# Three rows of w2 loaded ahead of the first K unit, and b1 loaded in one transfer, in a one-core decode kernel

## The chip, the cores and the metric

The kernel runs on one core of a Trainium2 chip. The metric is device time in microseconds (us). The kernel before takes 134.15 us (median of 5 runs, 134.06 to 134.36). A run of this program is called slow when it is over 1.5% above the fastest run of the same kernel; verdicts use the other runs, called fast. A change of under 2% counts as "same", so everything below is about tenths of a microsecond.

## The reference

x is normalised; an attention over the last 2048 cached positions (16 K/V heads, two batch rows, one query position) and a feed-forward part with a squared ReLU both read the normalised x; their results and x are added.

```python
xn = _layernorm(x, axis=-1)
return x + _A_ref(xn, A_k_cache, A_v_cache, A_wq, A_wo) + _B_ref(xn, B_w1, B_b1, B_w2, B_b2)
# _A_ref: q = xn @ wq; softmax(q k^T / sqrt(Dh)) v; @ wo       x is [2, 1, 576], Dh = 128
# _B_ref: h = xn @ w1 + b1; out = max(h, 0)^2 @ w2 + b2        w1 [576, 4608], w2 [4608, 576]
```

All of it is one position per batch row, so 53.6 MB of caches and weights pass through the core once, with little arithmetic on each byte.

## The kernel before

K and V come in eight units of 2 MB each; all large loads are issued by SyncE (`nc.sync`), the few small ones by ScalarE. w2's 4608 rows lie in four groups of 9 rows per partition. The parts that matter:

```python
    def issue_kv(tiles, cache, u, name, parts=1):      # [128 x 8192]: 32 x 4 pieces of DRAM
        tl = kvpool.tile([P, UE], BF16, tag="kv", name=f"{name}_{u}")
        v = unit_view(cache, u)
        ...                                            # nc.sync.dma_start(out=tl[...], in_=v[...])
    def issue_w2(g, r0, r1):
        if r0 == 0:
            w2_rows[g] = kvpool.tile([P, FR * D], BF16, tag="kv", name=f"w2_{g}")
        tl = w2_rows[g][:, r0 * D:r1 * D]
        rows = B_w2[g * HW:(g + 1) * HW, :].rearrange("(p r) n -> p (r n)", r=FR)
        nc.sync.dma_start(out=tl, in_=rows[:, r0 * D:r1 * D])
        ...

    nc.scalar.dma_start(out=x_sb[0:B, :], in_=x2d)
    for g in range(2):
        nc.scalar.dma_start(out=b1_sb[2 * g:2 * g + 2, :], in_=...)      # b1, two transfers
    for i in range(2):
        nc.scalar.dma_start(out=x_sb[B:B + 1, ...], in_=...)             # b2, two transfers
    ...
    for f in issue_kv(k_tiles, A_k_cache, 0, "k"):     # the first load of SyncE: K0
        f()
    issue_w(A_wq, "wq", QL)
    ...
    load_k(1); load_v(0); issue_w(B_w1, "w1", FL); load_k(2); load_v(1); load_k(3)
    for g in range(NG):
        transposes(0, g)                               # TensorE: K0
    q_all()                                            # TensorE: q = xn @ wq; frees wq's buffer for w1
    ...                                                # units 1 to 7
    W2P = [(0, 0, 9), (1, 0, 9), (2, 0, 9), (3, 0, 7), (3, 7, 9)]        # the last loads
    for w in W2P:
        issue_w2(*w)
    ...
    mlp_tail(*W2P[NG4][1:])                            # ends 3 us after the last load has landed
```

Of the kernel before, what the change touches and what calls it, by code (L numbers as in the profile page):

```python
# [8 lines left out]
F32 = mybir.dt.float32  # L9
BF16 = mybir.dt.bfloat16  # L10
# [6 lines left out]
def kernel(  # L17
# [14 lines left out]
    nc = tc.nc  # L32
    P = 128
    B, Sq, D = A_x.shape
# [24 lines left out]
    NG4 = 4  # L59
# [4 lines left out]
    HW = F // NG4  # L64
    HB = HW // 3
    FR = HW // P
# [7 lines left out]
    const = ctx.enter_context(tc.tile_pool(name="const", bufs=1))  # L74
# [7 lines left out]
    def pe_mm(out, **kw):  # L82
        return tc.keep_in_program_order(nc.tensor.matmul(out, **kw))  # L83
# [10 lines left out]
    k_tiles, v_tiles, w_tiles, wo_tiles, w2_tiles = {}, {}, {}, {}, {}  # L94

    def unit_view(cache, u):
        tq, b = divmod(u, B)
        return cache[b, tq * TH:(tq + 1) * TH, S0:Sk, :].rearrange("h (c j) d -> c h (j d)", c=CP)

    def issue_kv(tiles, cache, u, name, parts=1):  # L100
        tl = kvpool.tile([P, UE], BF16, tag="kv", name=f"{name}_{u}")
        v = unit_view(cache, u)
        n = UE // parts
        tiles[u] = tl
        return [lambda i=i: nc.sync.dma_start(out=tl[:, i * n:(i + 1) * n], in_=v[:, :, i * n:(i + 1) * n])  # L105
                for i in range(parts)]
# [7 lines left out]
    def issue_wo(t):  # L114
        if t == 0:
            wo_tiles["all"] = wbig.tile([P, B * WR, D], BF16, tag="wbig", name="wo_sb")
        tl = wo_tiles["all"][:, t * WR:(t + 1) * WR, :]
        n = P * WR
        nc.sync.dma_start(out=tl, in_=A_wo[t * n:(t + 1) * n, :].rearrange("(p r) n -> p r n", r=WR))
        wo_tiles[t] = tl  # L120
# [3 lines left out]
# [6 lines that stand above are left out]
        w2_tiles[(g, r0)] = tl  # L130
# [1 line left out]
    x_sb = const.tile([B + 1, D], BF16, name="x_sb")  # L132
    nc.scalar.dma_start(out=x_sb[0:B, :], in_=x2d)
    b1_sb = const.tile([NG4, HW], BF16, name="b1_sb")
    for g in range(2):
        nc.scalar.dma_start(out=b1_sb[2 * g:2 * g + 2, :], in_=B_b1[2 * g * HW:2 * (g + 1) * HW].rearrange("(g n) -> g n", g=2))
    for i in range(2):
        nc.scalar.dma_start(out=x_sb[B:B + 1, i * OH:(i + 1) * OH],
                            in_=B_b2[i * OH:(i + 1) * OH].rearrange("(o n) -> o n", o=1))
    eps_t = const.tile([B, 1], F32, name="eps_t")  # L140
    nc.vector.memset(eps_t[:], 1e-5)
    warm = const.tile([B, 122], F32, name="warm")
    nc.scalar.activation(out=warm[:, 0:1], in_=eps_t[:], func=ACT.Sqrt)
    for f in issue_kv(k_tiles, A_k_cache, 0, "k"):
        f()
    issue_w(A_wq, "wq", QL)
# [37 lines left out]
    for a in range(2):  # L184
        for r in range(NR2):
# [3 lines left out]
                          in_=pro_ps[:, 0:2 * NR2, :].rearrange("p (a r) b -> p r a b", a=2))  # L189
    nc.vector.tensor_copy(out=xnT[:, 1:HP:2, :, :],  # L190
                          in_=pro_ps[:].rearrange("p (a r) b -> p r a b", a=2)[:, 0:NR2 - 1, :, :])
# [16 lines left out]
                          in_=ident[0:TH, 0:TH].unsqueeze(1).to_broadcast([TH, NT * 32 // TH, TH]))  # L208
    par = const.tile([P, 2, 2, Dh // 2], BF16, name="par")
    for e in range(2):  # L210
        nc.gpsimd.tensor_copy(out=par[:, e, :, :],
                              in_=ident[:, e:Dh:2].unsqueeze(1).to_broadcast([P, 2, Dh // 2]))
# [3 lines left out]
    for k in range(2):  # L216
        for h in range(2):
            a = (h + k) % 2 * B
# [4 lines left out]
                          in_=ident[0:NG4, 0:NG4].unsqueeze(2).to_broadcast([NG4, NG4, B]))  # L223
# [6 lines left out]
    def out_acc(lhsT, rhs_of, start=False, stop=False):  # L230
        for i in range(2):
            pe_mm(out_ps[32 * i:32 * i + B, :], lhsT=lhsT, rhs=rhs_of(i * OH, (i + 1) * OH),
                  start=start, stop=stop, skip_group_check=True)
# [132 lines left out]
    def pv_out(u):  # L366
        tq, b = divmod(u, B)
        t, half = divmod(tq, 2)
        if u % (2 * B) == 0:
            sm_tiles[t] = psum.tile([P, B, Dh + 1], F32, tag="sm", name=f"sm_{t}")  # L370
        sm = sm_tiles[t]
        pe_mm(sm[half * (P // 2):(half + 1) * (P // 2), b, :],
                         lhsT=tohead[:].rearrange("p c x -> p (c x)"), rhs=acc_tiles.pop(u)[:], start=True, stop=True,
                         skip_group_check=True, tile_position=(0, half * (P // 2)))
        if u % (2 * B) == 2 * B - 1:
            ri = work.tile([P, B], F32, tag="ri", name=f"ri_{t}")
            pin(nc.vector.reciprocal(out=ri[:], in_=sm[:, :, Dh]))
            od = work.tile([P, B, DW, WR], F32, tag="od", bufs=1, name=f"od_{t}")
            for k in range(B):
                nc.vector.scalar_tensor_tensor(out=od[:, k, :, :],  # L380
                                               in0=sm[:, k, 0:Dh].rearrange("p (x r) -> p x r", x=DW),
                                               scalar=ri[:, k:k + 1],
                                               in1=own[:].unsqueeze(2).to_broadcast([P, DW, WR]),
                                               op0=ALU.mult, op1=ALU.mult)
            ws = work.tile([P, WR, B], BF16, tag="ws", name=f"ws_{t}")
            with nc.allow_low_precision(reason="sums of one value and zeros"):
                nc.vector.tensor_reduce(out=ws[:], in_=od[:].rearrange("p b x r -> p r b x"), axis=AX.X, op=ALU.add)  # L387
            wo_state[t] = ws

    def wo_acc(tq):  # L390
        ws = wo_state.pop(tq)
        wo_sb = wo_tiles.pop(tq)
        for r in range(WR):
            out_acc(ws[:, r, :], lambda a, z: wo_sb[:, r, a:z])

    mlp = {}
# [40 lines left out]
    def mlp_o(g, r0, r1):  # L437
        w2_sb = w2_tiles.pop((g, r0))
        for r in range(r0, r1):
            o = (r - r0) * D  # L440
            out_acc(mlp["h"][:, g * FR + r, :], lambda a, z: w2_sb[:, o + a:o + z], stop=(g == NG4 - 2 and r == r1 - 1))

    part = const.tile([B, D], F32, name="part")

    def mlp_tail(r0, r1):
        w2_sb = w2_tiles.pop((NG4 - 1, r0))
        for r in range(r0, r1):
            o = (r - r0) * D
            for i in range(4):
                pe_mm(mlp["out"][32 * i:32 * i + B, :], lhsT=mlp["h"][:, (NG4 - 1) * FR + r, :],  # L450
                                 rhs=w2_sb[:, o + i * OQ:o + (i + 1) * OQ], start=False, stop=(r == FR - 1),
                                 skip_group_check=True, tile_position=(0, 32 * i))

    def load_k(u):
        for f in issue_kv(k_tiles, A_k_cache, u, "k"):
            f()

    def load_v(u):
        for f in issue_kv(v_tiles, A_v_cache, u, "v"):
            f()  # L460

    W2P = [(0, 0, 9), (1, 0, 9), (2, 0, 9), (3, 0, 7), (3, 7, 9)]

    load_k(1)
    load_v(0)
# [13 lines left out]
    def step(u, p=None, o=None):  # L479
        if p is not None:  # L480
            pv_start(p)
        transposes(u, 0)
        softmax_max(u - 1)
        transposes(u, 1)
        softmax_exp(u - 1)
        transposes(u, 2)
        if p is not None:
            pv(p, 0)
        transposes(u, 3)
        if p is not None:  # L490
            pv(p, 1)
        softmax_tr(u - 1)
        if o is not None:
            pv_out(o)
        transposes(u, 4)
        scores(u, 0)
        for g in range(GW + 1, NG):
            transposes(u, g)
        for i in range(2, NR):
            if p is not None:  # L500
                pv(p, i)
        if p is not None:
            pv_mix(p)
        scores(u, 1)
# [13 lines left out]
    for u in range(2, NU - 1):  # L518
        step(u, u - 2 if u > 2 else None, u - 3 if u > 2 else None)
        if u == 2:  # L520
            out_acc(res_b[:], lambda a, z: x_sb[:, a:z], start=True)
        if u + 1 < NU - 1:
            load_v(u + 1)
        if u == 4:
            issue_wo(0)
        if u + 3 < NU:
            load_k(u + 3)
        if u == 5:
            load_v(NU - 1)
    issue_wo(1)  # L530
    for w in W2P:
        issue_w2(*w)
# [11 lines left out]
    wo_acc(0)  # L544
    pv_out(NU - 1)
    mlp_o(*W2P[0])
    wo_acc(1)
    for w in W2P[1:NG4 - 1]:
        mlp_o(*w)
# [3 lines left out]
    for i in range(4):  # L553
        pe_mm(mlp["out"][32 * i:32 * i + B, :], lhsT=ident_f[0:B, 0:B], rhs=part[:, i * OQ:(i + 1) * OQ],
              start=True, stop=False, skip_group_check=True, tile_position=(0, 32 * i))
    mlp_tail(*W2P[NG4 - 1][1:])
    mlp_tail(*W2P[NG4][1:])

# [36 lines left out]
```

## Time and profile before

| | before |
|---|---|
| time, median of 5 | 134.15 us |
| span of the profiled run | 132.2 us |
| first packet of a large load | 2.13 us |
| marks of K0 / wq / V0, median of 16 | 7.97 / 18.89 / 28.70 us |
| marks of the last load: first, median, last | 127.22, 127.89, 129.09 us |
| from the last mark to the end of the span | 3.1 us |

A load is split over 16 DMA engines, and each sends a completion mark when its share has landed. The trace holds the time of each mark and the start, size and duration of each packet, but it does not say which engine a mark or packet belongs to. The spread of a load's 16 marks shows how far the engines are apart. The lines of the profile are in the prediction. Here is only the head, which the argument turns on, in stretches of half a microsecond; the last two columns are the DMA share and GB/s, with each packet counted where it starts:

```profile
1.60:2.10 0.50, 0.00 (x0) 0.00 (x0) 0.39 (x2) 0.00 (x0) 0.50 (x3) 1.00 0.04 5
2.10:2.60 0.50, 0.00 (x0) 0.00 (x0) 0.40 (x3) 0.03 (x1) 0.50 (x1) 1.00 1.84 492
2.60:3.10 0.50, 0.00 (x0) 0.00 (x0) 0.49 (x3) 0.50 (x1) 0.34 (x1) 1.00 0.08 33
3.10:3.60 0.50, 0.00 (x0) 0.00 (x0) 0.44 (x4) 0.50 (x1) 0.00 (x0) 1.00 1.24 524
```

Until 2.1 us only x moves (5 GB/s). Then 15 of the 16 engines start one large K packet each (492), and in the next stretch only the last of them does (33), because those first packets take about 1 us instead of 0.61.

### The profile page before, as it was taken

To read this page: it belongs to the slowest core of one execution; us is meant where nothing else is said; L and a number is where in the kernel's file an instruction comes from. 1 tells how busy PE (TensorE), PEld (TensorE's weight loads), DVE (VectorE), ACT (ScalarE), POOL (GpSimd) and SP (SyncE) were. 2 spreads that over 40 slices of the span, in tenths; PEclk is the share of its full clock that TensorE was granted. 3 is DMA by queue.
4 is the path that set the end of the run, shared out by engine and by line. 5 is a ranking of instruction groups with operands and counts; after the bars stand their busy time and mean duration, and the time that the engine had idled before them with its cause. 6 is when DMAs were issued, how large, how long until landed. Compare 5 with 4: busy or idle time off the path is not lost.

```text
span 132.2 us, 2040 instructions
## 1 busy us (share of the span) xinstructions
PE 89.0 (67%) x830; PEld 54.7 (41%) x830; DVE 59.1 (45%) x150; ACT 44.2 (33%) x64; POOL 7.7 (6%) x26
## 2 busy tenths in 40 slices
PE   0069319789862967879889389789303996399761
PEld 0059202639521354744466064466003661155540
DVE  6944400224640019246675823778800358644011
ACT  2705401015700226438457145357100751200011
POOL 7700000001000001000010000010000000000000
PEclk9999995955999599689999977999985699959999
DMA  4999989999998999999999999999999999999950
GB/s 154 389 451 479 413 382 431 431 484 477 439 404 350 436 416 441 426 446 416 431 431 426 436 421 439 426 429 431 428 441 416 446 423 422 429 420 433 419 238 1
DMA packets 3632, 53.74 MB, mean 406 GB/s; under 512 B 412, under 2 KB 420, under 8 KB 680
## 3 DMA queue, kind: packets, MB, share of 16 engines
q1 hardware_dynamic: 3604, 53.61, 95.2%
q8 instruction: 6, 0.10, 0.3%
q10 hardware_dynamic: 20, 0.01, 0.0%
q14 instruction: 2, 0.02, 0.0%
HBM read 53.62 MB, written 0.00 MB: 405 GB/s over the span
## 4 chain that ended last, share of the span: by engine, by line
DMA 72%; PE 20%; DVE 2%; ACT 2%; issue 1%; SPq 1%; DVEq 0%; ACTq 0%
DMA k<-in_A_k_cache_dram 44%; DMA w<-in_B_w_dram 14%; DMA wq_sb<-in_A_wq_dram 13%; PE kT_ps L86 10%; PE sc_ps L83 4%; PE q_ps L83 3%; PE pv_ps L83 2%; PE qs_ps L83 1%; DVE kT L286 1%; ACT kT L284 1%; ACT pr L323 1%; PE sm L83 1%; DVE qrow L250 1%; SPq L105 0%; DVE qz L266 0%
## 5 line engine op out<-in xcount | busy, mean ns | idle before, releaser
L86 PE MATMUL kT_ps<-ident_f,k 128*128 128x128 f32 x256 | 41.4, 319 | 12.6 <-DMA k<-in_A_k_cache_dram 12.1
L284 ACT COPY kT<-kT_ps 128x1024 bf16<-128x1024 bf16 x32 | 31.9, 1011 | 36.8 <-PE kT_ps L86 34.0
L86 PEld LDWEIGHTS kT_ps<-ident_f,k 128*128 128x128 f32 x256 | 34.4, 165 | 21.9 <-issue 16.6
L286 DVE COPY kT<-kT_ps 128x1024 bf16<-128x1024 bf16 x32 | 22.1, 691 | 31.9 <-PE kT_ps L86 31.8
L83 PE MATMUL sc_ps<-kT,qz 128*32 128x512 bf16 x128 | 10.7, 418 | 4.5 <-DVE kT L286 2.8
L83 PE MATMUL pv_ps<-v,pT 128*32 128x512 bf16 x128 | 11.7, 435 | 1.0 <-DVE acc L358 0.8
L312 POOL PARTITION_ALL_REDUCE gmax<-m x8 | 2.9, 365 | 103.1 <-DVE m L310 103.1
L323 ACT ACTIVATE pr<-sc_ps,nb 128x512 bf16<-128x512 f32 x8 | 5.5, 687 | 7.9 <-DVE nb L320 7.9
L83 PEld LDWEIGHTS <-xnT 128*4 128x4 bf16 x90 | 2.9, 105 | 11.6 <-issue 11.0
L308 DVE TENSOR_REDUCE mx<-sc_ps 128x1 f32<-128x512 f32 x8 | 5.5, 683 | 3.1 <-PE sc_ps L83 3.1
L83 PE MATMUL q_ps<-wq_sb,xnT 128*4 128x512 bf16 x36 | 3.7, 592 | 4.5 <-DMA wq_sb<-in_A_wq_dram 4.5
L83 PEld LDWEIGHTS <-qz 128*32 128x32 bf16 x128 | 2.3, 98 | 10.1 <-DVE kT L286 6.3
L83 PE MATMUL h_ps<-w_sb,xnT 128*4 128x384 bf16 x54 | 3.9, 420 | 3.4 <-DMA w_sb<-in_B_w_dram 3.4
L358 DVE SCALAR_TENSOR_TENSOR mix<-pv_ps,own_j,mix 128x128 f32<-128x128 f32 x16 | 5.6, 352 | 0.6
L329 DVE STREAM_TRANSPOSE pT<-pr 128x512 bf16<-128x512 bf16 x8 | 5.6, 702 | 0.2 <-ACT pr L323 0.2
L86 PE MATMUL pro_ps<-ident,xs 2*128 2x2 bf16 x10 | 0.6, 164 | 7.6 <-DVE xs L180 7.6
L83 PE MATMUL out_ps<-wo_sb,ws 128*2 128x288 bf16 x64 | 5.1, 323 | 0.3 <-DVE ws L387 0.3
L83 PEld LDWEIGHTS <-pT 128*32 128x32 bf16 x128 | 2.9, 98 | 5.9 <-issue 3.5
L551 ACT COPY part<-out_ps 2x288 f32<-2x288 f32 x1 | 0.4, 389 | 13.5 <-PE out_ps L83 13.5
L83 PE MATMUL sm<-acc,tohead 128*64 128x129 f32 x16 | 3.7, 313 | 1.8 <-DVE acc L358 1.8
L431 DVE TENSOR_TENSOR hs<-hT_ps,hodd 128x20 f32<-128x20 f32 (+1 forms) x4 | 0.5, 172 | 9.2 <-ACT hodd L428 9.2
L83 PE MATMUL out_ps<-w,hT_sb 128*2 128x288 bf16 x54 | 3.8, 286 | 1.1 <-DMA w<-in_B_w_dram 1.1
(78 smaller groups left out, 58.2 us busy)
## 6 DMA issues: line engine op xcount, KB each, us to landing
k<-in_A_k_cache_dram SPq DMA_DIRECT2D x8, 2048.0 KB, 7.7
v<-in_A_v_cache_dram SPq DMA_DIRECT2D x8, 2048.0 KB, 16.9
w_sb<-in_B_w_dram SPq DMA_DIRECT2D x1, 5184.0 KB, 19.3
wq_sb<-in_A_wq_dram SPq DMA_DIRECT2D x1, 4608.0 KB
wo_sb<-in_A_wo_dram SPq DMA_DIRECT2D x2, 2304.0 KB
w<-in_B_w_dram SPq DMA_DIRECT2D x3, 1296.0 KB, 27.2
w<-in_B_w_dram SPq DMA_DIRECT2D x1, 1008.0 KB
w<-in_B_w_dram SPq DMA_DIRECT2D x1, 288.0 KB
```

What stands on the lines that cost most here:

```text
L83: return tc.keep_in_program_order(nc.tensor.matmul(out, **kw))
L86: return tc.keep_in_program_order(nc.tensor.transpose(**kw))
L250: nc.vector.tensor_copy(out=qrow[:, 0, :], in_=q_ps[0][0:RB, :])
L284: pin(nc.scalar.copy(out=dst, in_=src))
L286: pin(nc.vector.tensor_copy(out=dst, in_=src))
L308: pin(nc.vector.tensor_reduce(out=mx[:], in_=sc_ps, axis=AX.X, op=ALU.max))
L312: nc.gpsimd.partition_all_reduce(gmax[:], m2[:], channels=P, reduce_op=ReduceOp.max)
L323: pin(nc.scalar.activation(out=pr[:], in_=sc_ps, func=ACT.Exp, bias=nb[:], scale=scale, accum_out=acc[:, Dh:Dh + 1]))
L329: pin(nc.vector.transpose(out=pT[:].rearrange("p t m -> p (t m)"), in_=pr[:]))
L358: op = nc.vector.scalar_tensor_tensor(out=nx, in0=pv_ps[:, j, :], scalar=own_j[:, j:j + 1], in1=acc, op0=ALU.mult, op1=ALU.add)
L431: nc.vector.tensor_tensor(out=hs[:].rearrange("p (g r) b -> p r g b", g=NG4)[:, r0:r0 + n, g:g + 2, :], in0=even[:, :, g:g + 2, :], in1=od ...
L551: cp(out=part[:, i * OH:(i + 1) * OH], in_=out_ps[32 * i:32 * i + B, :])
```

## The change

Its intent is to fill the idle head of the load queue. Three rows of w2's group 2 (3,456 B a partition, 442 KB) are loaded ahead of K0 into a buffer of their own. They are multiplied in the middle, where TensorE has time, and the last loads are shorter by as much. Besides, b1 comes in one transfer instead of two. (The widths 80 and 178 only keep the following buffers aligned. Two lines are left out below: that of the buffer of width 178, and the one that sets the last product of the sum, which is now row R1 - 1 of group G1.)

```diff
-    for g in range(2):
-        nc.scalar.dma_start(out=b1_sb[2 * g:2 * g + 2, :], in_=B_b1[...].rearrange("(g n) -> g n", g=2))
+    nc.scalar.dma_start(out=b1_sb[:], in_=B_b1.rearrange("(g n) -> g n", g=NG4))
@@
+    G1 = NG4 - 2
+    R1 = FR - 3
+    w2_first = const.tile([P, (FR - R1) * D + 80], BF16, name="w2_first")
+    nc.sync.dma_start(out=w2_first[:, 0:(FR - R1) * D],
+                      in_=B_w2[G1 * HW:(G1 + 1) * HW, :].rearrange("(p r) n -> p (r n)", r=FR)[:, R1 * D:FR * D])
+    w2_tiles[(G1, R1)] = w2_first
     for f in issue_kv(k_tiles, A_k_cache, 0, "k"):
@@
-    W2P = [(0, 0, 9), (1, 0, 9), (2, 0, 9), (3, 0, 7), (3, 7, 9)]
+    W2P = [(0, 0, 9), (1, 0, 9), (G1, 0, R1), (3, 0, 7), (3, 7, 9)]
@@
         if u == 2:
             out_acc(res_b[:], lambda a, z: x_sb[:, a:z], start=True)
+            mlp_o(G1, R1, FR)
```

More of the change, by code (lines that the diff above doesn't have):

```diff
@@ L134 @@
     b1_sb = const.tile([NG4, HW], BF16, name="b1_sb")
-    for g in range(2):
-        nc.scalar.dma_start(out=b1_sb[2 * g:2 * g + 2, :], in_=B_b1[2 * g * HW:2 * (g + 1) * HW].rearrange("(g n) -> g n", g=2))
+    nc.scalar.dma_start(out=b1_sb[:], in_=B_b1.rearrange("(g n) -> g n", g=NG4))
     for i in range(2):
@@ L141 @@
     nc.vector.memset(eps_t[:], 1e-5)
-    warm = const.tile([B, 122], F32, name="warm")
+    warm = const.tile([B, 178], F32, name="warm")
     nc.scalar.activation(out=warm[:, 0:1], in_=eps_t[:], func=ACT.Sqrt)
+    G1 = NG4 - 2
[4 more added lines that the diff above has]
+    w2_tiles[(G1, R1)] = w2_first
     for f in issue_kv(k_tiles, A_k_cache, 0, "k"):
@@ L440, in mlp_o @@
             o = (r - r0) * D
-            out_acc(mlp["h"][:, g * FR + r, :], lambda a, z: w2_sb[:, o + a:o + z], stop=(g == NG4 - 2 and r == r1 - 1))
+            out_acc(mlp["h"][:, g * FR + r, :], lambda a, z: w2_sb[:, o + a:o + z], stop=(g == G1 and r == R1 - 1))
     part = const.tile([B, D], F32, name="part")
```

## The prediction

> **What bounds the kernel now.** I read the page first: the slices, the queues and the chain that ended last.
>
> ```profile
> PE 89.0 (67%) x830; PEld 54.7 (41%) x830; DVE 59.1 (45%) x150; ACT 44.2 (33%) x64; POOL 7.7 (6%) x26
> ...
> DMA  4999989999998999999999999999999999999950
> GB/s 154 389 451 479 413 382 431 431 484 477 439 404 350 436 416 441 426 446 416 431 431 426 436 421 439 426 429 431 428 441 416 446 423 422 429 420 433 419 238 1
> ...
> q1 hardware_dynamic: 3604, 53.61, 95.2%
> ...
> HBM read 53.62 MB, written 0.00 MB: 405 GB/s over the span
> ## 4 chain that ended last, share of the span: by engine, by line
> DMA 72%; PE 20%; DVE 2%; ACT 2%; issue 1%; SPq 1%; DVEq 0%; ACTq 0%
> ```
>
> TensorE is idle a third of the span; the one load queue (q1) is busy 95% of it, and only the first and the last slices are poor. So the loads are the bound, and the rest of the question is whether their queue ever runs dry. Busy time by stretch, whose last two columns are the DMA share and GB/s:
>
> ```profile
> 2.10:127.00 124.90, 87.43 (x786) 53.97 (x786) 56.91 (x143) 43.31 (x61) 6.14 (x19) 0.88 1.01 428
> ...
> 45.00:115.00 70.00, 50.70 (x425) 30.30 (x419) 38.32 (x92) 30.47 (x43) 2.56 (x7) 0.89 1.01 430
> ...
> 127.00:129.10 2.10, 1.30 (x42) 0.64 (x37) 0.45 (x1) 0.39 (x1) 0.00 (x0) 1.00 0.31 125
> 129.10:132.20 3.10, 0.30 (x8) 0.10 (x7) 0.59 (x2) 0.54 (x2) 0.00 (x0) 1.00 0.00 1
> ```
>
> From 2.10 to 127.00 us the queue moves 428 GB/s at a share of 1.01: saturated. Low single slices (350 at 40 us) are large packets that are counted where they start. The packet records confirm it: median 611 ns for a 16,384 B packet, 389 for 10,368 B, 93 for 2,304 B, that is about 8 ns + bytes / 27.2 per ns. One engine carries a sixteenth of every load: 128 x 611 + 24 x 389 + 16 x 686 + 8 x 1364 + 8 x 1533 + 8 x 305 + 8 x 93 ns = 124.9 us. The first load packet starts at 2.13 us, so an engine that never waits ends at about 127.0; the 16 completion marks of the last load run from 127.22 to 129.09 us. The quickest engine thus hardly waited at all, and the slowest is 1.9 us behind it, which was mostly put there in the middle: six 16 KB instruction fetches (q8, 0.9 us each) share the same engines. The end of the chain in order of time:
>
> ```profile
> 109.99 19.10 DMA w<-in_B_w_dram
> 129.09 0.04 issue
> 129.13 0.40 PE tail_ps L83 x8
> 129.53 0.05 ACT fin_sb L563
> ```
>
> The time is therefore: start of the load stream, plus about 125 us of packets, plus the lag of the slowest engine, plus 3.1 us from its last mark (129.09) to the end (132.2). A reordering of loads that moves the same bytes can only touch the first term (and, by accident, the third). The start, from the timeline:
>
> ```profile
> 0.72 0.63 SPq L105 DMA_DIRECT2D k<-in_A_k_cache_dram  x1
> 0.72 0.54 ACTq L133 DMA_DIRECT2D x_sb<-in_A_x_dram  x1
> ...
> 1.30 0.63 ACTq L136 DMA_DIRECT2D b_sb<-in_B_b_dram  x2
> 1.40 0.57 SPq L110 DMA_DIRECT2D wq_sb<-in_A_wq_dram  x1
> ```
>
> SyncE can issue at 0.72 us; the first K load takes 0.63 us to issue; its first packet starts at 2.13 us. And those first sixteen packets take 0.67 to 1.10 us instead of 0.61, all ending near 3.2 us, whether they started at 2.13 or at 2.63: data really flow only from about 3.2 - 0.6 = 2.6 us. Beside it, x (two rows) is issued at the same 0.72 us, and its packets start at 1.65 us and take 0.07 and 0.24 us.
>
> **What the Trainium skill says.** (1) "DMA: Bandwidth & Descriptors", section "Where 436 GB/s comes from", puts the ceiling of one core's ports at 435 GB/s; the 430 of the middle stretch agrees, so no order of the loads makes the stream itself faster. (2) The same page, "Latency and other measured facts", gives a first byte about 600 ns after a hardware-generated DMA. Here x needs 0.93 us from the start of its issue (0.39 from the end of it), K 1.41 us (0.78 from the end): K is slower than the page's figure, x near it, and the difference is what this change can win. (3) "Why a DMA increments its semaphore by 16 and not by 1" says that a DMA of few rows uses as many engines as divide its row count, the lowest-numbered ones. Then the two b1 loads of two rows each lie on the same two engines, and one load of four rows on four. The trace shows two 2,304 B packets at a time, at 3.9 and at 5.8 us, but does not name engines. (4) "Issuing engines are not separate DMA queues" says that issuing from several engines only saves issue time; b1's packets waiting until 3.9 and 5.8 us after issues at 1.30 and 1.57 us show them sharing with K.
>
> **The change, part by part.**
> *Three rows of w2 ahead of K.* 3 x 576 x 2 B = 3,456 B a partition, 442,368 B in all: at 430 GB/s 1.03 us at the head of the queue, and the same 1.03 us gone from near its end (the load of group 2 has six rows instead of nine). These cancel exactly: every load between lands 1.03 us later, less what is won at the head. What does not cancel is the head. The later loads of w2 are issued in 0.33 us each, those of K in 0.54 us (medians of the tile view). The first issue of an engine costs more: 0.63 against 0.54 for K, so 0.09; I take 0.42 us, end of issue 1.14 us. The first packet then starts 0.39 us (as x) to 0.78 us (as K) later: 1.53 to 1.92, middle 1.73 us, against 2.13: 0.40 us won. If a small, plain load also lacks K's slow first packets, data flow up to 0.4 us earlier still; if instead it starts as late as K, nothing is won. K itself is issued by 0.42 + 0.06 + 0.54 us after 0.72, 1.74 us, and its packets can start at 1.74 + 0.78 = 2.5 us. Eight w2 packets on an engine take 8 x (8 + 3456 / 27.2) = 1.08 us and last until about 2.9 us, so K follows without a hole. That is why three rows are about the right size.
> *Its cost.* A partition of group 2 now comes in two packets (3,456 and 6,912 B) instead of one: 8 more packets on an engine at 8 ns, and one more completion mark at 9 ns: 0.07 us.
> *b1 in one transfer.* ACT issues one DMA less, about 0.3 us at 1.3 to 1.9 us, in front of a table load that nothing on the path awaits: 0. Two engines carry one 93 ns packet instead of two. If one of those two is the slowest of all, 0.09 us are won, else nothing; I count 0.02.
> *Six products in the middle.* Three rows x two matmuls on h, right after the u = 2 step, at about 58 us. The 54 such matmuls near the end are 3.8 us busy, so six are 0.4 us. hT is written at 49.6 us and the rows landed long before: no wait. SyncE's next loads are issued well ahead (the K unit issued at 56.83 us lands only about 76 us), so 0.4 us of TensorE there reaches nothing. The 0.4 us leave the group-2 products, after which TensorE waits for the next load anyway: 0.
> *The early chain.* K0 and wq land about 0.6 us later (1.03 + 0.07 - 0.4), so q and the release of wq's buffer are as much later: the w1 load is issued at 23.6 instead of 22.97 us. The queue then holds work until 28.4 us (V0's landing), itself later by as much, so 5.4 us of backlog stay. No hole.
> *Sum.* -0.40 + 0.07 - 0.02 = -0.35, and a share of the doubtful 0.4 us of faster first packets, 0.1: -0.45 us. 134.29 - 0.45 = 133.85 us.
>
> **The rivals.**
> *The start is fixed.* The first packets wait for something that no form of load shortens (descriptor generation, the first access). For it: all sixteen end at one moment. Against: x's packets are done at 1.9 us. Then only the cost stays: 134.29 + 0.07 = 134.35.
> *The full 1.03 us.* If w2's data flowed entirely in time that is idle now, K would not be later at all. It would need data from 1.57 us on (2.6 - 1.03), with the first packet a good 0.8 us after the start of the issue. Then about 133.3. Possible, not likely.
> *The later K unit is a new wait.* Compute starts on K0 later, buffers come free later, the queue runs dry: up to +0.6 us, about 134.9. Against: 5.4 us of backlog at 23 us, and a stream that never stops after.
> *The lag of the slowest engine moves.* Instruction fetches fall on other packets or engines when the program and its timing change: plus or minus some 0.3 us, either way.
>
> **Range and chances.** 133.85, and between the full win and the fixed start with some lag: 133.4 to 134.4. The three runs before lie within 0.2 us. Two per cent are 2.7 us, more than the whole idle head: faster 0.01, within 0.98, slower 0.01.
>
> **What would show it.** The w2 issue at 0.72 us takes 0.4 us and the first load packet starts near 1.7 us; K's issue follows near 1.2 us; K0's first transposes begin about 0.6 us later than 8.44 us, wq's products later than 19.20 by as much; the saturated share stays near 1.01 in the middle; the last landing is near 128.65 instead of 129.09, and from it to the end are 3.1 us still. I am wrong if the first packet is at 2.1 us again, if the issue of w1 falls behind V0's landing, or if the last landing moves by something other than the head did.

## The result, and the profile after

The changed kernel took 134.12 us (median of 5: 136.9, 134.07, 133.76, 134.15, 134.12) against 134.15 for the kernel before. The ratio is 0.9984, with a 95% interval of 0.9966 to 1.0002. A ratio here is the mean time of one kernel's fast runs over that of the other's of the same rounds, so it is not quite the ratio of the medians; a sixth fast run of the changed kernel, 133.78 us, counts in it. That is about 0.2 us less, where 0.45 was foretold, and an interval that just includes no change at all.

More telling than the median is the one run of 136.9 us: the kernel before had nothing of the kind. The profile that came with the result was of that run. The changed kernel was therefore run again, twice, and the second time (133.72 us) gave the profile that is compared here. First the issues of the head:

```profile
0.72 0.40 SPq L146 DMA_DIRECT2D w_first<-in_B_w_dram  x1
0.72 0.55 ACTq L133 DMA_DIRECT2D x_sb<-in_A_x_dram  x1
1.18 0.62 SPq L105 DMA_DIRECT2D k<-in_A_k_cache_dram  x1
1.30 0.26 ACTq L135 DMA_DIRECT2D b_sb<-in_B_b_dram  x1
```

The early load is issued in 0.40 us, where K0 took 0.63; K0's issue follows at 1.18 us. The stretches of the head in the same run:

```profile
1.60:2.10 0.50, 0.00 (x0) 0.00 (x0) 0.39 (x2) 0.00 (x0) 0.50 (x3) 1.00 0.91 164
2.10:2.60 0.50, 0.00 (x0) 0.00 (x0) 0.40 (x3) 0.20 (x1) 0.50 (x1) 1.00 0.73 166
2.60:3.10 0.50, 0.00 (x0) 0.00 (x0) 0.49 (x3) 0.50 (x1) 0.34 (x1) 1.00 0.96 373
3.10:3.60 0.50, 0.00 (x0) 0.00 (x0) 0.44 (x4) 0.50 (x1) 0.00 (x0) 1.00 1.68 697
```

The stretch from 1.60 us, almost empty before, now moves 164 GB/s, with the first packet at 1.73 us. But until 2.6 us the rate is far under the 430 of the steady stream: the small packets too are slow at first (up to 0.84 us instead of 0.135). The middle, and the use of the early rows (from the stretches and the tile view):

```profile
45.00:115.00 70.00, 50.56 (x441) 30.23 (x433) 37.52 (x91) 30.39 (x43) 2.56 (x7) 0.91 1.01 430
```

```profile
L83 PE MATMUL out_ps<-w_first,hT_sb x6: 283/284/286, 59.6 to 59.9; 128*2 128x288 bf16 x6
```

The middle is saturated at 430 GB/s as before, and the six products start within 0.3 us at 59.6 us. The waits for wq and for the last load, from the chain that ended last:

```profile
1.84 18.11 DMA wq_sb<-in_A_wq_dram
...
110.79 17.98 DMA w<-in_B_w_dram
128.81 0.40 PE tail_ps L83 x8
```

The last load has landed by 128.77 us, against 129.09 before: 0.3 us are won in this run.

### The profile page after: what moved, and what is told of

Same layout as the page of the kernel before. It is cut to its first block, busy times and chain, and to the rows that moved or that the text cites. A ratio compares the mean times of both kernels' runs of the same rounds, so it can differ in the third digit from the quotient of the medians.

```text
span 135.1 us, 2040 instructions
## 1 busy us (share of the span) xinstructions
PE 90.2 (67%) x830; PEld 57.0 (42%) x830; DVE 59.1 (44%) x150; ACT 44.4 (33%) x64; POOL 7.7 (6%) x26
## 4 chain that ended last, share of the span: by engine, by line
DMA 69%; PE 23%; DVE 2%; ACT 2%; issue 1%; SPq 1%; DVEq 0%; ACTq 0%
DMA k<-in_A_k_cache_dram 41%; DMA wq_sb<-in_A_wq_dram 15%; DMA w<-in_B_w_dram 13%; PE kT_ps L86 10%; PE sc_ps L83 4%; PE q_ps L83 3%; PE qs_ps L83 3%; PE pv_ps L83 2%; DVE kT L291 1%; PE sm L83 1%; ACT kT L289 1%; ACT pr L328 1%; DVE qrow L255 1%; SPq L105 0%; DVE qz L271 0%
## 5 line engine op out<-in xcount | busy, mean ns | idle before, releaser
L86 PEld LDWEIGHTS kT_ps<-ident_f,k 128*128 128x128 f32 x256 | 35.3, 168 | 27.3 <-issue 19.9
L83 PEld LDWEIGHTS <-ws 128*2 128x2 bf16 x64 | 3.2, 100 | 2.9 <-DVE ws L392 0.6
L83 PEld LDWEIGHTS qs_ps<-sel_q,qrow 100*128 100x128 f32 x16 | 3.5, 330 | 1.8 <-issue 1.8
L360 DVE TENSOR_SCALAR mix<-pv_ps,own_j 128x128 f32<-128x128 f32 x8 | 2.8, 344 | 3.2 <-PE pv_ps L83 3.2
```

What stands on the lines that cost most here:

```text
L83: return tc.keep_in_program_order(nc.tensor.matmul(out, **kw))
L86: return tc.keep_in_program_order(nc.tensor.transpose(**kw))
L360: op = nc.vector.tensor_scalar(out=nx, in0=pv_ps[:, j, :], scalar1=own_j[:, j:j + 1], scalar2=None, op0=ALU.mult)
```

## The experiments

All comparisons are with the kernel before on the same chip and in the same rounds. "Early rows" are rows of w2 loaded at the head.

### 1. Each part alone, and the early rows moved from the head

Four kernels on one chip. The first is the changed kernel again.

> The changed kernel again, for a profile in the fast state. Theory A (the early plain load starts the stream sooner): first load packet near 1.74 us, K0's first completion mark about 0.6 us later than in the kernel before (7.80), the last landing about 0.2 to 0.45 us earlier than 129.09, time ratio 0.997 to 0.999. Theory B (the start is fixed, the difference is chance): last landing within 0.1 us of before, ratio 0.9995 to 1.001.

The second is the kernel before with the one transfer for b1 only.

> The kernel before with b1 in one transfer, w2 untouched. Theory A: nothing to see, ratio 0.999 to 1.0005, the first load packet still near 2.13 us. Rival C (the two b1 loads on the same two engines cost more than their 93 ns packets, so that merging them is what gains): ratio 0.997 to 0.9985, with the last landing 0.2 us earlier or more.

The third is the changed kernel with b1 in two transfers again.

> The changed kernel with b1 in two transfers as before. Theory A: as the changed kernel, ratio 0.997 to 0.999, first load packet near 1.74 us. Rival C: as the kernel before, ratio 0.9995 to 1.001.

The fourth loads the early rows after V0:

```diff
-    nc.sync.dma_start(out=w2_first[:, ...], in_=B_w2[...])      # ahead of K0
     ...
     load_v(0)
+    nc.sync.dma_start(out=w2_first[:, ...], in_=B_w2[...])
     issue_w(B_w1, "w1", FL)
```

> The changed kernel, but the three rows are loaded after V0 instead of ahead of K0, still into their own home and used in the middle. Theory A: K0 is the first load again, its first packet near 2.13 us, only the 0.07 us of extra packets is left, ratio 0.9995 to 1.001. Rival D (the gain comes from the shorter tail or the use in the middle, not from the head): ratio 0.997 to 0.999, as the changed kernel.

| run | times, us | ratio, 95% | first packet | last load: median, last mark |
|---|---|---|---|---|
| changed kernel (1) | 134.49, 133.85, 135.25, 134.92, 135.28, 133.80 | 1.0031, 0.9996 to 1.0066 | 1.73 | 127.61, 129.57 |
| b1 only (2) | 134.02 to 134.43 | 1.0009, 0.9994 to 1.0025 | 2.12 | 127.80, 128.99 |
| w2 only (3) | 134.13, 133.82, 134.08, 134.18, 135.42, 135.77 | 1.0029, 0.9987 to 1.0071 | 1.73 | 127.88, 129.10 |
| after V0 (4) | 133.87 to 134.07 | 0.9987, 0.9974 to 1.0000 | 2.13 | 127.87, 129.04 |

Rival C falls: b1 in one transfer gains nothing that these runs can see, and w2 alone behaves like the whole change. The start is not fixed either (theory B): the first packet moves by 0.4 us with the kind of the first load, and only with that. The ratio of the fourth kernel missed the range that theory A gave it (0.9987 instead of 0.9995 or more). Its interval touches 1 and its marks at the end are those of the kernel before within 0.05 us, so rival D is neither shown nor fully excluded by it: in time alone, this control gains as much as the change did in its first runs (0.9984). What the kernel does settle is that the buffer of its own and the products in the middle cost nothing visible.

My numbers for the first and third runs were wrong, in a way that nobody had expected. Both kernels have runs as low as 133.8 us and others 1 to 2 us higher. Here are wq's landing and the end of the chain in the first kernel's profile, a fast run of 134.49 us:

```profile
1.83 18.68 DMA wq_sb<-in_A_wq_dram
...
111.50 18.07 DMA w<-in_B_w_dram
129.61 0.40 PE tail_ps L83 x8
```

Against the good run above, wq is 0.57 us later and the end 0.80 us later. The marks tell why wq is later: in the good run K0's last three marks are at 8.95, 9.00 and 9.02 us; here they are at 8.98, 9.05 and 9.62. A single engine is late. In the third kernel's profile it is later still (8.91, 8.97, 10.72), and wq waits for it:

```profile
1.83 19.79 DMA wq_sb<-in_A_wq_dram
```

That run still took only 134.13 us, because the engines drift up to 1.9 us apart in the course of any run (in the kernel before too: 127.22 to 129.09 us in the last load). The trace shows what moves them. It has eight instruction fetches, six of 16,384 B (about 0.9 us each) and two of 8,192 B (0.31 us). In the kernel before, the marks after each fetch show one more engine fallen back, by 1.2 to 1.5 us after a large one and by 0.6 to 0.8 us after a small one, and each time another engine: at the end eight of them are 0.8 to 1.9 us behind the first.

A late engine costs time only as far as it ends behind the others that drifted. So a late K0 engine alone explains the later wq, but not yet the later end. In the first kernel's profile all 16 marks still lie within 2.0 us of each other in the load that ends at 125.67 us. The last fetch, at 124.88 us, meets an engine that has already finished its part of that load, and in the last load fifteen marks lie at or before 128.77 us and one at 129.57. Two engines were 1.2 us behind when it came, one of them the late one of K0, and the trace does not tell which of the two it hit; the eighth kernel's profile, in the next study, does.

### 2. The length of the early load, another first load, and the small loads out of the way

The packet records show where the late engine loses its time. In steady state 16 packets are in flight, one an engine. In the third kernel's profile there are 15 from 3.3 to 4.1 us, between the end of one engine's early rows and its part of K0; then one of K0's packets takes 1.78 us instead of 0.61. So theory H says: in some runs one engine runs out of early packets before its part of K0 is ready. Four kernels on one chip: six early rows, and one early row (`R1 = FR - 6`, `R1 = FR - 1`);

> The changed kernel with six rows ahead of K0 instead of three: the early load lasts until about 4.6 us instead of 3.5. Theory H (in some runs one engine runs out of early packets before its part of K0 is ready and stands idle, 15 packets in flight instead of 16 from about 3.3 us): fewer or shorter holes, spread of the runs at most half of the changed kernel's 133.8 to 135.3, best run near 133.8. Rival I (the hole does not depend on how long the early load lasts): the same spread as the changed kernel.

> One row ahead of K0: its packets end near 2.4 us, before K0's can start. Theory H: holes on most engines for some tenths of a us, the head wins at most 0.2 us, K0's first completion mark near 7.80 + 0.36 + 0.07 - 0.2 = 8.0 us; late single engines in some runs, 134.0 to 135. Rival I: as the changed kernel, best run 133.8.

wq ahead of K0, without any early rows:

```diff
-    for f in issue_kv(k_tiles, A_k_cache, 0, "k"):
-        f()
     issue_w(A_wq, "wq", QL)
+    for f in issue_kv(k_tiles, A_k_cache, 0, "k"):
+        f()
@@
+    q_all()
     for g in range(NG):
         transposes(0, g)
-    q_all()
```

> The kernel before with wq loaded ahead of K0, and q computed ahead of K0's transposes; w2 and b1 untouched. wq is a plain load too, with 36,864 B packets that last 11 us. Theory A plus H: first load packet near 1.75 us as with the three rows, no hole behind it, no added packets: ratio 0.996 to 0.998, every run between 133.6 and 134.0. Rival I (late engines come with any other load ahead of K0): single runs over 134.5.

and the changed kernel with the loads of b1 and b2 moved behind ScalarE's copies of K0's transposes (the order of the neighbouring ScalarE instructions pinned as it was), so that only x runs beside the early rows.

> The changed kernel, but b1 and the two halves of b2 are issued by ScalarE only after its copies of K0's transposes, at about 16 us, so that nothing but x runs beside the early load. Theory J (the small loads in ScalarE's queue hold up one engine's part of K0): no late engine, every run between 133.6 and 134.1. Theory H: late engines as in the changed kernel, some runs over 134.4.

| run | times, us | ratio, 95% | K0: 13th, last mark | last load: median, last mark |
|---|---|---|---|---|
| six rows (5) | 133.79, 134.48, 133.93, 133.92, 134.05, 134.25 | 0.9997, 0.9980 to 1.0013 | 9.97, 10.33 | 127.52, 128.84 |
| one row (6) | 134.42, 135.05, 134.77, 134.49, 134.52, 134.47 | 1.0041, 1.0024 to 1.0058 | 8.87, 9.36 | 128.50, 129.47 |
| wq first (7) | 133.75, 134.22, 134.28, 134.18, 134.12, 134.33 | 1.0002, 0.9987 to 1.0017 | 18.92, 19.23 | 127.96, 128.81 |
| small loads late (8) | 134.77, 133.90, 135.69, 133.82, 133.76, 133.77 | 1.0013, 0.9972 to 1.0054 | 8.73, 9.72 | 127.58, 129.67 |

One early row makes the hole plain, and on nearly all engines. Its head:

```profile
1.60:2.10 0.50, 0.00 (x0) 0.00 (x0) 0.40 (x2) 0.00 (x0) 0.50 (x3) 1.00 0.46 67
2.10:2.60 0.50, 0.00 (x0) 0.00 (x0) 0.40 (x3) 0.20 (x1) 0.50 (x1) 1.00 0.73 251
2.60:3.10 0.50, 0.00 (x0) 0.00 (x0) 0.49 (x3) 0.50 (x1) 0.35 (x1) 1.00 2.36 524
3.10:3.60 0.50, 0.00 (x0) 0.00 (x0) 0.44 (x4) 0.50 (x1) 0.00 (x0) 1.00 0.00 0
```

The row's packets end near 2.6 us, where only 3 packets are in flight. Then every engine starts its first K packet (524), and none starts a second one before 3.6 us, because these first packets take 0.9 to 1.4 us. So the slow first packets of a stream are paid twice here, and this is the only kernel of all that is clearly slower than the one before. With six rows the late runs are gone but for one of 134.48 us, and one engine is 0.3 us late instead of 0.6 to 1.8. Six runs are few, though: at three late ones in ten, none over 134.6 us would come up with a chance of 0.7^6 = 0.12. Both kernels fit theory H, and the empty stretch above shows that the length makes a difference at the short end: rival I falls there.

Theory J falls: with the small loads out of the way an engine is still late, and two of six runs are over 134.7 us. At the end of that profile, 15 marks of the last load are at or before 128.56 us and one is at 129.67. Here the marks can be followed. The late engine is 1.30 us behind the first at K0 and still 1.31 in the w2 load whose first mark is at 121.60 us, where fetches have put five others 1.6 to 1.8 us behind, so it costs nothing yet. The last fetch, at 124.11 us, hits this engine: afterwards no mark is 1.3 us behind and one is 2.86. So the late end of this run took two things, an engine late at the head and a fetch on the same engine. In the third kernel's profile the engine that is 2.12 us behind at K0 gets no fetch and ends 1.98 behind, and the run takes 134.13 us. The chain of the eighth kernel:

```profile
1.84 18.78 DMA wq_sb<-in_A_wq_dram
...
110.82 18.85 DMA w<-in_B_w_dram
129.71 0.52 PE tail_ps L83 x7
```

wq first did not do what I expected. It has no late run, but it is not faster either (1.0002 instead of 0.996 to 0.998). Its first packet starts at 1.73 us, yet V0's median mark is at 28.51 us, only about 0.1 us earlier than with K0 first. Its first sixteen 36,864 B packets take 1.77 to 2.53 us instead of 1.36, so most of the head start is lost in the first packets. Why five of its runs are near 134.2 while the profiled one took 133.75 stays open.

### 3. What follows the early rows

Three kernels on another chip: the changed kernel again, to count its late runs beside the others;

> The changed kernel once more, on the chip and beside the runs of the next two, to count its late runs. Theory H (a third of its runs has one engine whose part of K0 starts late): one to four of six runs over 134.4 us, the others 133.7 to 134.2; in a late profile the last completion mark of K0 lies 0.5 us or more behind the others. Theory B (those runs were a chip's mood): all six within 133.9 to 134.4.

the early rows issued by ScalarE ahead of x, so that K0 is SyncE's first load and both queues hold packets at once;

```diff
+    nc.scalar.dma_start(out=w2_first[:, ...], in_=B_w2[...])
     nc.scalar.dma_start(out=x_sb[0:B, :], in_=x2d)
     ...
-    nc.sync.dma_start(out=w2_first[:, ...], in_=B_w2[...])
```

> The changed kernel, but the three early rows are issued first from ScalarE's queue, x behind them, so that K0 is SyncE's first load again and can be ready from 2.13 us while the early rows still run. Theory H: no engine runs out of packets between them, no run over 134.3, ratio 0.997 to 0.9985, the median of the last load's marks near 127.6. Rival K (the engines that are late are late for any small packets at the start): late runs as in the changed kernel.

and the changed kernel with wq, not K0, behind the early rows. The diff is that of "wq first", on top of the change.

> The changed kernel with wq as the load behind the three rows and K0 after it, q computed ahead of K0's transposes. wq is issued in about 0.33 us, K0 in 0.6. Theory H, if the lateness comes from the slow issue of K0: few or no late engines, wq's last mark within 0.5 us of its thirteenth, no run over 134.4, ratio 0.997 to 0.999. Rival K: late runs as in the changed kernel, the late engine seen on wq's marks instead of K0's.

The last one was run once more, on a further chip:

> The last kernel again, for the count: five runs without a late one still happen 0.13 of the time by chance if a third of the runs were late. Theory H: again no run over 134.3, ratio 0.997 to 0.999, wq's last mark within 0.5 us of its thirteenth. Rival K (the early rows alone make engines late): one or more runs over 134.4, the late engine on wq's marks.

| run | times, us | ratio, 95% | 13th, last mark of the load behind the rows | last load: median, last mark |
|---|---|---|---|---|
| changed kernel (9) | 133.72, 134.05, 133.80, 136.59 (slow), 133.87, 133.96 | 0.9986, 0.9973 to 0.9998 | K0: 8.91, 9.02 | 127.68, 128.77 |
| rows on ScalarE (10) | 133.99 to 134.14 | 0.9995, 0.9983 to 1.0007 | K0: 9.03, 9.18 | 127.62, 128.98 |
| rows, wq, K0 (11) | 133.76, 133.87, 133.79, 133.96, 133.79 | 0.9979, 0.9967 to 0.9991 | wq: 14.89, 15.09 | 127.45, 128.83 |
| rows, wq, K0 again (12) | 133.76, 134.00, 133.79, 133.70, 133.90, 133.66 | 0.9974, 0.9959 to 0.9989 | wq: 14.93, 14.98 | 127.67, 128.80 |

With wq behind the rows no mark is far behind the others (although the eleventh profile too has 15 packets in flight from 3.2 to 3.6 us), and the chain of the eleventh kernel shows wq as the second load and the end as in the good runs:

```profile
1.18 13.91 DMA wq_sb<-in_A_wq_dram
...
111.63 17.20 DMA w<-in_B_w_dram
128.87 0.40 PE tail_ps L83 x8
```

wq's issue here takes 0.41 us, where K0's takes 0.62. This order is clearly faster than the kernel before in both studies, by 0.3 us, and it has the best median of all versions: 133.79 and 133.78 us. Against the fast runs of the changed kernel on the same chip (mean 133.88) its mean of 133.83 is no clear gain; what it lacks is the late runs.

The count over all runs, with the line at 134.6 us, which none of the 49 runs of the kernel before reached (highest 134.55):

| order at the head of SyncE's queue | runs over 134.6 us |
|---|---|
| K0 first (before, b1 only, rows after V0, rows on ScalarE) | 0 of 65 |
| wq first | 0 of 6 |
| three rows, then K0 (the change, w2 only, small loads late) | 9 of 30 |
| six rows, then K0 | 0 of 6 |
| one row, then K0 | 2 of 6 |
| three rows, then wq | 0 of 11 |

If three in ten were the rate everywhere, eleven runs without a late one would come up with a chance of 0.7^11 = 0.02. Two of the nine (136.9 and 136.59) count as slow; without them it is 7 of 28, and 0.75^11 = 0.04. So rival K (the early rows alone make engines late) is unlikely, and which load follows seems to matter. Whether ready packets in another queue help is not shown: the tenth kernel has no late run in five and no gain that these runs can see (0.9995).

## Why the prediction was right or wrong

**The bound: right.** In every good run the stream is saturated at 430 GB/s in the middle, and from the last mark to the end it is 3.1 us (128.77 to 131.9). Only the head and the lag of the slowest engine moved.

**The start of the stream: right to 0.02 us.** I had the issue at 0.42 us and the first packet at 1.73; they are 0.40 and 1.73. K0's issue follows at 1.18 us (1.20 foretold).

**"A share of the doubtful 0.4 us of faster first packets, 0.1": wrong in sign.** It is a term of the sum. I had hoped that a small, plain load would be spared the slow first packets of K0. It is not, and part of the slowness seems to be paid again when K0 begins. In the first 8 us an engine's packets of SyncE's queue take together 0.40 us more than their usual length where K0 comes first (mean of three profiles: 0.48, 0.30, 0.41). With three rows first they take 0.55 us more (mean of the four fast profiles of the changed kernel, w2 only and small loads late: 0.56, 0.56, 0.53, 0.56). So about 0.15 us of the 0.40 are given back at once. V0's median mark says the same. It is 28.61 us in the mean of those three profiles with K0 first, and 29.37 in the good run of the changed kernel. Less the 8 x 135 + 9 ns that the early rows take, that is 28.28: 0.33 us won, not 0.5.

**The cost of splitting: right by its packets.** 262 + 135 ns instead of 389 for the two parts, times eight, and a mark of 9 ns: 0.07 us.

**b1: not contradicted.** 0.02 were foretold, too little to be measured, and nothing measurable came (ratio 1.0009 alone).

**The products in the middle and the early chain: right.** The products run at 59.6 us without a wait, and w1 is issued at 24.0 us (23.6 foretold), 5.0 us ahead of V0's first mark at 29.05 (5.4 foretold): no hole.

**"K follows without a hole": wrong.** This is the step that cost most. I had the rows' packets last until about 2.9 us and K0 able to start at 2.5. In fact the rows last until about 3.6, and K0's first packet starts at 3.18 (the good run). On most engines they do follow without a hole. But in three of the four fast profiles one engine is late at K0. It gets its first K0 packet up to 0.9 us late, and that packet itself can take up to 1.8 us. In the slow profile it was about 2 us late. Nine of 30 runs end over 134.6 us. I computed the mean engine; the end is set by the last one. That a hand-over between two loads has its own spread from engine to engine is what I had no view for: the kernel before shows only a first load that starts on an empty core, and loads that were queued long before.

**The sum.** (134.29 - 0.45 is 133.84, and 134.29 + 0.07 is 134.36; the prediction has both off by 0.01.) In a good run the last landing is 0.32 us earlier (0.44 foretold: 128.65 against 128.77 measured), and late engines take part of this back. So 0.2 us remained in the first five runs, nothing or less on another chip (ratio 1.0031), and 0.2 on a third (0.9986, without its one slow run). That the first median, 134.12, lies within my 133.4 to 134.4 is partly luck: on the second chip the median of the same kernel is 134.70. The rival "the lag of the slowest engine moves" was the right worry, and instruction fetches are half of it, as it said: the eighth kernel's profile shows the last fetch on the engine that K0 had left late. I put it at plus or minus 0.3 us either way. It is one-sided, because the change adds a late engine, and goes up to 1.6 us in the fast runs (135.77 in the third kernel against 134.13 before) and 2.8 in the slow one.

**What stays open.** Why K0, and not wq, leaves an engine late. The two loads differ in their access pattern (K0's DRAM side is in 32 x 4 pieces), in the time of issue (0.62 against 0.41 us) and in packet size (16,384 against 36,864 B), and no run separates the three. Theory H's reason, that one engine's part of K0 is not ready yet, is not shown either: with one row, after the same issue of K0 (1.18 to 1.80 us), all 16 engines had started K0 by 3.1 us, while the hole with three rows lasts from 3.3 to 4.1. Nor does the trace say whether it is always the same engine.

## What to carry to other kernels

In this kernel, which the load stream bounds, the free time was before its first packet, and the first load decided how long that was: a plain [128 x n] load (w2's rows or wq) starts 0.4 us sooner here than K0, whose DRAM side is in two-level pieces. Whatever is put there must last until the next load runs on all 16 engines: look at the last mark, not the first or the mean. Here the order with the quickly issued wq as the second load was one without late runs (0 of 11). Judge a change of tenths of a microsecond by many runs and by the spread of the marks, since a median can hide that three runs in ten got worse.

## What the Trainium skill lacked or had wrong

- "DMA: Bandwidth & Descriptors", section "Latency and other measured facts", gives one first-byte time for hardware-generated DMAs, about 600 ns. Here the first packet starts 0.61 us after the end of the issue for a plain load (0.40 us of issue), 0.79 us for K0 (0.63 us of issue) and 0.39 us for x. Counted from the start of the issue it is 1.01, 1.41 and 0.93 us; the page's figure agrees only with the first, and only from the issue's end.
- The same page has nothing on the first packets of a stream. Sixteen first K packets take 0.67 to 1.10 us instead of 0.61, and they are slow again after a pause (0.91 to 1.42 us in the kernel with one early row).
- Its "Rules for kernel authors" do not say that a hand-over from a short load to the next can leave one engine empty while the other fifteen run on (15 packets in flight from 3.3 to 4.1 us, up to 1.8 us lost on that engine in a fast run).
- "Runtime: NRT & Kernel Launch", section "Instruction fetch mechanics", calls the cost of a 16 KiB instruction fetch "mostly hidden"; it does not speak of the load stream. Here six such packets in a queue of their own take about 0.9 us each on the engines that also carry the loads, and the engines end 1.9 us apart (127.22 to 129.09 us in the kernel before).
- The ceiling of 435 GB/s in the section "Where 436 GB/s comes from" of the DMA page holds: 430 GB/s in the middle stretch before and after. The same section says that for transfers from HBM the lower figure of about 358 binds; in these loads it did not.
